# Softmax's division moved from GpSimd to ScalarE, a short token tile packed into one product, and a new split of the last columns

## The chip, the cores and the metric

The kernel runs on one core of a Trainium2 chip. The metric is the device time of one execution in microseconds (us), the median over several runs. The core has five engines with queues of their own: PE (TensorE, matrix products), DVE (VectorE), ACT (ScalarE), POOL (GpSimd) and SP (SyncE, which here issues every DMA).

## The reference

Three blocks follow each other, for 4 batches of 576 tokens with 512 features:

```
scores = scale * q @ k.T            8 heads of 64; heads 0-3 see a window of 32 tokens,
attn   = softmax(masked scores)     heads 4-7 every 4th of 128 tokens
x      = attn @ v
xk, xr = mu * x + (1 - mu) * x_prev (two sets of mu)
x      = sigmoid(xr @ w_r) * (relu(xk @ w_k)**2 @ w_v)
u      = x + (x.T @ U @ V).T        U is 576 x 32, V is 32 x 576: a mix over tokens
out    = u + relu(u @ w_ch1) @ w_ch2
```

Weights come as 64-bit floats and are turned into 32-bit ones on the chip.

## The kernel before, in words

**Order of the work.** Nothing is issued straight away. The builder records operations with the engine, a cost in ns, and the keys that they read and write (op, L124). A planner (plan, L130) then plays the five queues forward, 24 times with ranks from a backward pass, keeps the shortest order, and the operations are issued in that order (L1305 to L1311). Each engine then runs its own list in order. So the costs that the code writes decide which operation stands ahead of which. `lock=True` makes the planner keep a GpSimd and a VectorE operation from overlapping. Where the planner sees TensorE idle for more than 600 ns ahead of a product, it puts matmuls on a tile of zeros there (L279 to L289, issued at L1308), as many as fill 0.7 of the gap at 0.453 ns a column.

**Attention.** 32 units (one pair of heads, one part of the tokens). The first four run alone (attend, L578), the others in twos (attend2, L650), one pair at each "visit" between products of the second block. A unit's scores go to PSUM (qk, L597 or L676), VectorE takes the negated minimum of each group of 64 columns (low, L537), ScalarE the exponential of each group with its row's bias and sum (exp, L546), VectorE the reciprocals of the sums (inv, L551 and L552), GpSimd multiplies all groups by them in one instruction (norm, L557), TensorE transposes (L628, L714), ScalarE copies the transposes out (pts, L632, L720, by the helper at L352), and TensorE multiplies by v (pv, L640, L732). A single unit issues norm twice, for 64 and for 320 columns; a pair issues it once for each head, for 320 or 256 columns.

**Second block.** Chunks of 288 tokens. The first chunk uses whole 32-bit weights (L812, L828), the others split weights and inputs into a high and a low part and do three products for each (L815 to L817). Weights are converted by one ScalarE pass (L385) and four VectorE passes (L386, L387, L389, L392). GpSimd takes the low parts of the inputs (L347).

**Mix over tokens.** For each batch the 576 tokens are five tiles of 128, the last of them only 64 tokens long. y_tr (L902) transposes a tile (L908), ScalarE writes its high part, VectorE its low part. In the short tile GpSimd sets rows 64 to 127 of both parts to zero (L916). u_mm (L919) multiplies each tile's high and low part by U's tile, 512 columns each (L926, L927).

**Third block.** Groups of 256 or 512 tokens. ch1 makes the hidden part (L1036 to L1038), ch2 (L1100) multiplies by w_ch2 into four PSUM banks (L1113 to L1115). After the last step VectorE adds u to each bank (L1133) and SP sends it out (L1136). In the last group the fourth bank is added and sent in two halves of 256 columns, both after the bank's last product.

Of the kernel before, what the change touches and what calls it, by code (L numbers as in the profile page):

```python
# [12 lines left out]
ALU = mybir.AluOpType  # L13
# [3 lines left out]
P = 128  # L17
# [51 lines left out]
SLACK_PE = 100.0  # L69

LATE = 1500.0
FILL, FILL_FROM, FILL_NS = 0.7, 600.0, 0.453
PLAN_PRINT = None
PASSES = 24
RATE = 285.0
# [3 lines left out]
def tile_attention_mix_channel(  # L79
# [18 lines left out]
    def f32(ap):  # L98
        return ap.bitcast(F32)
# [30 lines left out]
    def plan():  # L130
# [149 lines left out]
        for o in order:  # L280
            if o.eng != "PE":
                continue
            for x in [x for x in o.first if x.home is ps][:1] or [k[0] for k in o.w if o.spare][:1]:
                ends = sorted((max(u.done for u in y.ops) for y in x.line[: x.at]), reverse=True)
                room = o.at - max([idle_from, *ends[x.bufs - 1 : x.bufs]])
                if room > FILL_FROM:
                    wide = CW if x in o.first else CW - HS
                    o.before = (x, wide, int(FILL * room / (FILL_NS * wide)))
            idle_from = o.at + o.ns  # L289
        if PLAN_PRINT:  # L290
            PLAN_PRINT(order)
# [44 lines left out]
    def dma(nbytes, fn, r, w):  # L336
        op("SP", 415, fn, r, w, size=nbytes)
# [214 lines left out]
        nc.vector.reciprocal(sm[:, :n], sm[:, :n])  # L552

    def norm(pr, d, sm, i, n, d_to=None):
        src = pr[:, d : d + n * KW].rearrange("p (w k) -> p w k", k=KW)
        dst = src if d_to is None else pr[:, d_to : d_to + n * KW].rearrange("p (w k) -> p w k", k=KW)
        nc.gpsimd.tensor_tensor(out=dst, in0=src, in1=sm[:, i : i + n].unsqueeze(2).to_broadcast([P, n, KW]), op=ALU.mult)  # L557

    LOW, EXP, NORM = 150, 330, 1.69 * KW

    def x_out(ov, q, part, b):

# [15 lines left out]
    def attend(u):  # L578
# [41 lines left out]
        op("DVE", 6 * LOW, lows, [(x,) for x in sc] + [("cst",)], [(pr,), (mn,)], 170)  # L620
        op("ACT", 5 * EXP, exps, [(pr,), (mn,)], [(pr,), (sm,)], 190, mode="exp")
        op("DVE", 260, lambda: inv(sm(), 5), [(sm,)], [(sm,)], 80, lock=True)
        op("POOL", 360 + 6 * NORM, norms, [(pr,), (sm,)], [(pr,)], 40, lock=True)
        yield

        def tr():
# [23 lines left out]
    def attend2(ua, ub):  # L650
# [33 lines left out]
        for e in range(2):  # L684
            first_, own = (ns - 4, 0) if e else (0, 4)
            base = e * ns * KW

            def lows(e=e, first_=first_, own=own, base=base):
                for i in range(4):
                    low(sc[e](), i * KW, pr(), base + (first_ + i) * KW, mk[i // 2], mn[e](), first_ + i)  # L690
                if nw == 10:
                    for f in range(2):
                        low(sc[f](), (4 + e) * KW, pr(), base + own * KW, mk[2], mn[e](), own, head(f))

            def exps(e=e, base=base):
# [206 lines left out]
    def y_tr(b, t, tag):  # L902
        n = min(P, S - t * P)
        pt = bank(tag)

        def tr():
            for p in range(NPAIR):
                nc.tensor.transpose(pt()[:n, p * P : (p + 1) * P], yb[b]()[:, p, t * P : t * P + n], ident)  # L908

        pe(4 * 108, tr, [(yb[b],), ("cst",)], [(pt,)], "tr")  # L910
        hi, lo = Lazy([P, DM], F32R, "w32", "yh", 3), Lazy([P, DM], F32R, "w32", "yl", 3)
        copy(DM, lambda: hi()[:n], lambda: pt()[:n], [(pt,)], [(hi,)], psum=True)
        sub("DVE", DM, lambda: lo()[:n], lambda: pt()[:n], lambda: f32(hi()[:n]), [(pt,), (hi,)], [(lo,)], psum=True)
        if n < P:
            for x in (hi, lo):
                op("POOL", 250, lambda x=x: nc.gpsimd.memset(f32(x()[n:]), 0.0), [], [(x, "rest")], 40)  # L916
        yhl[b, t] = (hi, lo, P)

    def u_mm(b, t, tag):  # L919
        if t == 0:  # L920
            uacc[b] = bank(tag)
        acc = uacc[b]
        hi, lo, n = yhl.pop((b, t))
# [5 lines left out]
        pe(2 * 233, run, [(hi,), (lo,), (hi, "rest"), (lo, "rest")] + [("us", g) for g in range(4)], [(acc,)], "f32r", 400)  # L929
# [166 lines left out]
        return hh, hl, [(t, key) for t in (hh, hl) for key in "io"]  # L1096

    accs = {}

    def ch2(g, j, hid):  # L1100
        hh, hl, kh = hid
        t0, n = GROUPS[g]
        if j == 0:
            accs[g] = [bank("S") for _ in range(4)]
        for o in range(4):
            acc = accs[g][o]

            def run(o=o, acc=acc):
                a = acc()[:, :n]
                for e in range(2):  # L1110
                    wh, wl = (t()[:, o * P : (o + 1) * P] for t in rows2_w[2 * j + e])
                    xh, xl = (t()[:, e * n : (e + 1) * n] for t in (hh, hl))
                    nc.tensor.matmul(a, lhsT=wh, rhs=xh, start=(j == 0 and e == 0), stop=False)  # L1113
                    nc.tensor.matmul(a, lhsT=wl, rhs=xh, start=False, stop=False)  # L1114
                    nc.tensor.matmul(a, lhsT=wh, rhs=xl, start=False, stop=(j == 7 and e == 1))  # L1115

            pe(6 * (MMW if g else MMQ), run, [(t,) for e in range(2) for t in rows2_w[2 * j + e]] + kh, [(acc,)], "f32r")
        if j < 7:
            return
        last = g == len(GROUPS) - 1  # L1120
        for o in range(4):
# [4 lines left out]
            else:  # L1126
                dma(P * n * 4, lambda o=o, ot=ot: nc.sync.dma_start(ot(), uf[:, o, t0 : t0 + n]),
                    [("uf", c, o) for c in range(t0 // HS, (t0 + n - 1) // HS + 1)], [(ot,)])
                u_, ku = ot, (ot,)
            step = Q if last and o == 3 else n  # L1130
            for c0 in range(0, n, step):
                c = slice(c0, c0 + step)
                dve(step, lambda acc=acc, ot=ot, u_=u_, c=c: nc.vector.tensor_tensor(  # L1133
                    out=ot()[:, c], in0=acc()[:, c], in1=u_()[:, c], op=ALU.add),
                    [(acc,), ku], [(ot, c0) if last else (ot,)], two=True, psum=True)
                dma(P * step * 4, lambda o=o, ot=ot, c=c: nc.sync.dma_start(  # L1136
                    out[o, :, t0 + c.start : t0 + c.stop], ot()[:, c]), [(ot, c0) if last else (ot,)], [("out", g, o, c0)])


# [263 lines left out]
```

## Time and profile before

| what | value |
|---|---|
| median of 3 runs | 758.99 us (758.56 to 760.91) |
| the profiled execution | 759.92 us |
| its span in the trace | 758.1 us |
| PE, DVE, ACT, POOL busy, share of the span | 98%, 75%, 52%, 51% |

The profiled execution is one run of the program with the profiler on. Its span is the time from the first to the last record, and the rest of its time lies around the span. Busy time of an engine is the union of its records; a matmul's record includes its way through the array, so 98% for PE says that a product was under way nearly always, and not how dense the products were. Starts of neighbouring products say that.

### The profile page before, as it was taken

How to read it: one execution, taken by the hardware profiler on the slowest of the kernel's cores; microseconds unless marked ns; L12 is line 12 of the kernel's file. 1: busy time of each engine (PE TensorE's matmuls, PEld its weight loads, DVE VectorE, ACT ScalarE, POOL GpSimd, SP SyncE). 2: the span in 40 equal slices, each digit the busy share in tenths (PEclk: the TensorE clock that was granted, in tenths of full speed). 3: DMA queues.
4: the chain of work that ended last, by engine and by line, in shares of the span. 5: the costliest groups of instructions: out<-in, count | busy, mean ns of one | idle time of the engine just before them, and what ended most of it. 6: DMA issues, size and time to landing. Idle time of an engine off the chain costs nothing.

```text
span 758.1 us, 18341 instructions
## 1 busy us (share of the span) xinstructions
PE 739.3 (98%) x6921; PEld 677.6 (89%) x6921; DVE 567.9 (75%) x1335; ACT 393.1 (52%) x995; POOL 388.3 (51%) x408
## 2 busy tenths in 40 slices
PE   8899999999999999999999999999999999999997
PEld 6667999999999999999999998888988989898986
DVE  5999989999898845775677778675888765575632
ACT  4578795767585746372555454343453434343310
POOL 1331464646464635273765677544677554456500
PEclk9999999999999999999999999999999999999999
DMA  9767346776756540557543252132532212042001
GB/s 333 238 255 246 133 148 192 267 248 202 267 179 205 176 157 1 196 160 225 178 153 100 94 181 100 57 125 83 171 102 84 85 56 84 29 140 70 15 1 55
DMA packets 53223, 109.77 MB, mean 145 GB/s; under 512 B 5648, under 2 KB 15888, under 8 KB 53136
## 3 DMA queue, kind: packets, MB, share of 16 engines
q1 hardware_dynamic: 53136, 108.62, 43.4%
q8 instruction: 54, 0.88, 0.5%
q14 instruction: 33, 0.27, 0.1%
HBM read 86.05 MB, written 22.54 MB: 143 GB/s over the span
## 4 chain that ended last, share of the span: by engine, by line
PE 83%; DVE 7%; POOL 3%; issue 3%; DMA 3%; ACT 1%; SPq 0%; DVEq 0%; POOLq 0%; ACTq 0%
PE psM L815 10%; PE psM L816 9%; PE psM L817 9%; PE psS L1115 8%; PE psS L1113 8%; PE psS L1114 8%; PE psM L1036 7%; PE psM L1037 6%; PE psM L1038 6%; PE psM L812 4%; PE psS L732 2%; PE psS L676 1%; DMA uf<-us 1%; POOL cl L347 1%; DVE ok L1073 1%
## 5 line engine op out<-in xcount | busy, mean ns | idle before, releaser
L347 POOL TENSOR_TENSOR cl<-sums,ch 128x512 fp32r<-128x512 f32 x72 | 98.6, 1369 | 93.5 <-ACT ch L352 62.4
L1113 PE MATMUL psS<-hh,rh 128*128 128x512 f32 (+1 forms) x320 | 119.3, 373 | 1.8 <-DVE us L949 1.5
L1115 PE MATMUL psS<-hl,rh 128*128 128x512 f32 (+1 forms) x320 | 119.4, 373 | 0.4 <-DVE hl L1051 0.3
L1114 PE MATMUL psS<-hh,rl 128*128 128x512 f32 (+1 forms) x320 | 118.9, 372 | 0.0
L352 ACT ACTIVATE ch<-sums 128x512 fp32r<-128x512 f32 (+1 forms) x104 | 57.5, 562 | 104.7 <-DVE sums L472 97.0
L815 PE MATMUL psM<-xk,wh 128*128 128x288 f32 x336 | 101.7, 303 | 0.0
L816 PE MATMUL psM<-xk,wl 128*128 128x288 f32 x336 | 99.5, 296 | 0.0
L817 PE MATMUL psM<-xk,wh 128*128 128x288 f32 x336 | 99.3, 295 | 0.0
L347 POOL TENSOR_TENSOR cl<-st,ch 128x256 fp32r<-128x256 f32 x80 | 66.9, 852 | 50.9 <-PE psM L1038 34.7
L472 DVE TENSOR_TENSOR sums<-st 128x256 f32<-128x256 f32 (+1 forms) x144 | 86.2, 646 | 7.8 <-POOL cl L347 3.9
L347 POOL TENSOR_TENSOR xk<-m,xk 128x288 fp32r<-128x288 f32 x56 | 54.8, 992 | 36.2 <-ACT xk L352 18.8
L1115 PEld LDWEIGHTS psS<-hl,rh 128*128 128x128 f32 x320 | 60.3, 188 | 12.3 <-DVE hl L1093 1.0
L1113 PEld LDWEIGHTS psS<-hh,rh 128*128 128x128 f32 x320 | 60.3, 188 | 11.7 <-DVE us L949 1.7
L1114 PEld LDWEIGHTS psS<-hh,rl 128*128 128x128 f32 x320 | 60.3, 188 | 9.4
L815 PE MATMUL psM<-k2s,wh 128*128 128x288 f32 x224 | 67.2, 300 | 0.0
L816 PE MATMUL psM<-k2s,wl 128*128 128x288 f32 x224 | 66.1, 295 | 0.2 <-issue 0.2
L817 PE MATMUL psM<-k2s,wh 128*128 128x288 f32 x224 | 66.0, 295 | 0.0
L815 PEld LDWEIGHTS psM<-xk,wh 128*128 128x128 f32 x336 | 63.5, 189 | 0.7 <-DVE wl L349 0.2
L347 POOL TENSOR_TENSOR k2s<-k,k2s 128x288 fp32r<-128x288 f32 x49 | 45.1, 926 | 36.7 <-ACT k2s L352 34.2
L816 PEld LDWEIGHTS psM<-xk,wl 128*128 128x128 f32 x336 | 63.7, 190 | 0.1
L817 PEld LDWEIGHTS psM<-xk,wh 128*128 128x128 f32 x336 | 63.7, 190 | 0.0
L1093 DVE SCALAR_TENSOR_TENSOR hl<-ort,hh 128x512 fp32r<-128x512 f32 x32 | 26.0, 811 | 46.3 <-ACT hh L1092 46.2
(152 smaller groups left out, 2137.1 us busy)
## 6 DMA issues: line engine op xcount, KB each, us to landing
st<-w2f SPq DMA_DIRECT2D x96, 256.0 KB, 3.1
w<-w2raw SPq DMA_DIRECT2D x32, 512.0 KB, 5.1
w<-w1raw SPq DMA_DIRECT2D x20, 512.0 KB, 5.7
w2f<-w SPq DMA_DIRECT2D x32, 256.0 KB, 2.6
raw<-qk SPq DMA_DIRECT2D x16, 320.0 KB, 6.4
ytmp<-y SPq DMA_DIRECT2D x32, 144.0 KB, 2.6
yb<-ytmp SPq DMA_DIRECT2D x4, 1152.0 KB, 6.8
uf<-us SPq DMA_DIRECT2D x32, 144.0 KB, 1.9
```

Source lines behind the costliest of these rows:

```text
L347: op("POOL", t, lambda: nc.gpsimd.tensor_tensor(out=out_(), in0=a(), in1=b(), op=ALU.subtract), r, w, 40, lock=True)
L352: act(n, lambda: nc.scalar.activation(out_(), in_(), AF.Copy), r, w, psum, strided)
L472: dve(k * Q, lambda: nc.vector.tensor_tensor(out=q(sm_, n, k)(), in0=a(), in1=b(), op=op_), [(s1,), (s2,)], [(sm_, key)], two=True)
L815: nc.tensor.matmul(a, lhsT=wh, rhs=xh, start=start, stop=False)
L816: nc.tensor.matmul(a, lhsT=wl, rhs=xh, start=False, stop=False)
L817: nc.tensor.matmul(a, lhsT=wh, rhs=xl, start=False, stop=stop)
L1036: nc.tensor.matmul(a, lhsT=wh()[:, wi], rhs=xh()[:, ci], start=(k == 0), stop=False)
L1037: nc.tensor.matmul(a, lhsT=wl()[:, wi], rhs=xh()[:, ci], start=False, stop=False)
L1038: nc.tensor.matmul(a, lhsT=wh()[:, wi], rhs=xl()[:, ci], start=False, stop=(k == len(parts) - 1))
L1113: nc.tensor.matmul(a, lhsT=wh, rhs=xh, start=(j == 0 and e == 0), stop=False)
L1114: nc.tensor.matmul(a, lhsT=wl, rhs=xh, start=False, stop=False)
L1115: nc.tensor.matmul(a, lhsT=wh, rhs=xl, start=False, stop=(j == 7 and e == 1))
```

## The change

- The division: norm now issues one ScalarE copy per group of 64 columns, with the reciprocal as the copy's per-row scale. A single unit has 6 such copies, a pair's head 5 or 4. The planner counts 180 ns for one, on ACT; GpSimd has no part in it and the lock with VectorE falls away.
- The short token tile: its high part stays in rows 0 to 63, its low part is written to rows 64 to 127 of the same tile, and U's last 64 rows stand twice in U's tile. One product replaces two, and the zeros of L916 are gone.
- The end: in the last step of the last group the fourth bank's products are done for columns 0 to 383 and then for 384 to 511, and each part is added and sent by itself.
- Fill-in matmuls take 0.6 of a gap instead of 0.7, and half as many ahead of 7 us of the planner's time.

```diff
-FILL, FILL_FROM, FILL_NS = 0.7, 600.0, 0.453
+FILL, FILL_FROM, FILL_NS, FILL_COLD = 0.6, 600.0, 0.453, 7000.0
...
-                    o.before = (x, wide, int(FILL * room / (FILL_NS * wide)))
+                    pace = FILL_NS * (2 if o.at < FILL_COLD else 1)
+                    o.before = (x, wide, int(FILL * room / (pace * wide)))
...
-        nc.gpsimd.tensor_tensor(out=dst, in0=src, in1=sm[:, i : i + n].unsqueeze(2).to_broadcast([P, n, KW]), op=ALU.mult)
-    LOW, EXP, NORM = 150, 330, 1.69 * KW
+        for w in range(n):
+            to = (d if d_to is None else d_to) + w * KW
+            nc.scalar.activation(
+                pr[:, to : to + KW], pr[:, d + w * KW : d + (w + 1) * KW], AF.Copy, scale=sm[:, i + w : i + w + 1])
+    LOW, EXP, NORM = 150, 330, 180
...
-        op("POOL", 360 + 6 * NORM, norms, [(pr,), (sm,)], [(pr,)], 40, lock=True)
+        op("ACT", 6 * NORM, norms, [(pr,), (sm,)], [(pr,)], 140)
...
-            op("POOL", 180 + ns * NORM, lambda e=e, base=base: norm(pr(), base, sm[e](), 0, ns), kp + ks, kp, 40, lock=True)
+            op("ACT", ns * NORM, lambda e=e, base=base: norm(pr(), base, sm[e](), 0, ns), kp + ks, kp, 140)
...
-        sub("DVE", DM, lambda: lo()[:n], lambda: pt()[:n], lambda: f32(hi()[:n]), [(pt,), (hi,)], [(lo,)], psum=True)
-        if n < P:
-            for x in (hi, lo):
-                op("POOL", 250, lambda x=x: nc.gpsimd.memset(f32(x()[n:]), 0.0), [], [(x, "rest")], 40)
-        yhl[b, t] = (hi, lo, P)
+        to, rows = (lo, slice(0, n)) if n == P else (hi, slice(n, P))
+        sub("DVE", DM, lambda: to()[rows], lambda: pt()[:n], lambda: f32(hi()[:n]), [(pt,), (hi,)], [(to, "lo")], psum=True)
+        yhl[b, t] = (hi, lo) if n == P else (hi,)
...
-            nc.tensor.matmul(acc(), lhsT=us[:n, t, :], rhs=hi()[:n], start=(t == 0), stop=False)
-            nc.tensor.matmul(acc(), lhsT=us[:n, t, :], rhs=lo()[:n], start=False, stop=(t == NT - 1))
+            for i, y in enumerate(parts):
+                nc.tensor.matmul(acc(), lhsT=us[:, t, :], rhs=y(), start=(t == 0 and i == 0), stop=(t == NT - 1))
...
+    ENDS = ((0, 3 * Q // 2), (3 * Q // 2, 2 * Q))
...
-        for o in range(4):
+        end = g == len(GROUPS) - 1 and j == 7
+        for o, (c0, c1) in [(o, c) for o in range(4) for c in (ENDS if end and o == 3 else ((0, n),))]:
...
-            step = Q if last and o == 3 else n
-            for c0 in range(0, n, step):
+            for c0, c1 in ENDS if last and o == 3 else ((0, n),):
...
-    up[:S] = um
+    up[:S], up[S:] = um, um[S - NT * P :]
```

## Rows read from the trace of the kernel before

**Rows 1.** The page's busy times: engine, us (share of the span), instructions.

```profile
PE 739.3 (98%) x6921; PEld 677.6 (89%) x6921; DVE 567.9 (75%) x1335; ACT 393.1 (52%) x995; POOL 388.3 (51%) x408
```

**Rows 2.** Stretches: length, busy PE, PEld, DVE, ACT, POOL (count), granted clock, DMA share, GB/s.

```profile
12.00:16.00 4.00, 4.00 (x78) 2.90 (x74) 3.90 (x15) 3.06 (x15) 0.66 (x1) 1.00 1.03 390
...
20.00:40.00 20.00, 16.46 (x275) 12.40 (x274) 19.12 (x64) 11.94 (x40) 7.16 (x9) 1.00 0.81 256
...
60.00:80.00 20.00, 19.96 (x308) 15.88 (x315) 18.21 (x58) 16.84 (x45) 6.71 (x9) 1.00 0.78 250
...
100.00:104.00 4.00, 4.00 (x129) 3.79 (x122) 3.54 (x21) 4.00 (x12) 2.61 (x4) 0.61 0.51 132
```

**Rows 3.** Waits of PE: waiter, releaser, us in total, times, longest.

```profile
PE psS L628 <- POOL pr L557: 1.5, 2, 0.9
PE psS L732 <- ACT pts L352: 1.4, 1, 1.4
PE psS L714 <- POOL pr L557: 0.8, 1, 0.8
PE psS L927 <- POOL yl L916: 0.7, 1, 0.7
```

**Rows 4.** The chain that ended last, 0 to 56 us: start, us, what.

```profile
1.46 4.10 PE psS L1308 x9
...
20.85 0.81 DVE wx L386
...
33.90 0.77 DVE wx L386
...
45.66 10.22 PE psM L812 x40
```

**Rows 5.** Timeline of DVE and POOL, 24 to 30 us: start, us, engine, line.

```profile
24.57 0.42 DVE L386 TENSOR_SCALAR wx<-wx 128x512 f32<-128x512 f32 x1
...
28.20 0.84 DVE L386 TENSOR_SCALAR wx<-wx 128x512 f32<-128x512 f32 x1
...
27.67 1.09 POOL L557 TENSOR_TENSOR pr<-pr,sm 128x64 f32<-128x64 f32 x2 [0.33 <-DVE sm L552]
```

**Rows 6.** Groups: line, engine, operation, count | busy us, mean ns | idle before.

```profile
L546 ACT ACTIVATE pr<-pr,mn 128x64 f32<-128x64 f32 x144 | 48.1, 336 | 8.7 <-DVE mn L537 7.2 <-POOL pr L557 1.3
...
L352 ACT ACTIVATE ch<-st 128x256 fp32r<-128x256 f32 x80 | 28.7, 404 | 6.4 <-PE psM L816 4.1 <-PE psM L1038 2.3
...
L557 POOL TENSOR_TENSOR pr<-pr,sm 128x320 f32<-128x320 f32 (+2 forms) x36 | 26.3, 732 | 60.3 <-DVE sm L552 42.3 <-ACT wx L385 7.9 <-ACT pr L546 3.9
...
L352 ACT ACTIVATE rh<-st 128x512 fp32r<-128x512 f32 x16 | 9.7, 621 | 4.6 <-DMA st<-w2f 4.6
...
L926 PE MATMUL psS<-yh,us 128*128 128x512 f32 x10 | 4.1, 412 | 0.0
...
L916 POOL MEMSET yh<- 64x512 f32 x4 | 2.1, 522 | 0.6 <-PE psM L927 0.4
```

**Rows 7.** Timeline of ACT at the first exponentials.

```profile
6.44 0.35 ACT L546 ACTIVATE pr<-pr,mn 128x64 f32<-128x64 f32 x1 [4.41 <-DVE mn L537]
6.69 0.19 ACT L546 ACTIVATION_READ_ACCUMULATOR pr<-pr,mn 128x1 f32 x1
```

**Rows 8.** The first loads: issue, time to landing (last number), and the second unit's scores.

```profile
0.75 0.39 SPq L526 DMA_DIRECT2D raw<-qk  x1
...
raw<-qk SPq DMA_DIRECT2D x1, 320.0 KB, 3.3
...
9.02 0.50 PEld L597 LDWEIGHTS psS<-raw 64*32 64x32 f32 x40 [0.35 <-DMA raw<-qk]
```

**Rows 9.** The end: last piece of PE in the chain, then VectorE's adds and SP's issues.

```profile
753.69 0.24 PE psS L1115
...
753.95 0.76 DVE L1133 TENSOR_TENSOR ot<-psS,ug 128x256 f32<-128x256 f32 x2 [0.70 <-PE psS L1115]
...
753.28 1.94 SPq L1136 DMA_DIRECT2D out<-ot  x3
```

More of the change, by code (lines that the diff above doesn't have):

```diff
@@ L554, in norm @@
     def norm(pr, d, sm, i, n, d_to=None):
-        src = pr[:, d : d + n * KW].rearrange("p (w k) -> p w k", k=KW)
-        dst = src if d_to is None else pr[:, d_to : d_to + n * KW].rearrange("p (w k) -> p w k", k=KW)
-        nc.gpsimd.tensor_tensor(out=dst, in0=src, in1=sm[:, i : i + n].unsqueeze(2).to_broadcast([P, n, KW]), op=ALU.mult)
-    LOW, EXP, NORM = 150, 330, 1.69 * KW
+        for w in range(n):
[3 more added lines that the diff above has]
+    LOW, EXP, NORM = 150, 330, 180
     def x_out(ov, q, part, b):
@@ L922, in u_mm @@
         acc = uacc[b]
-        hi, lo, n = yhl.pop((b, t))
+        parts = yhl.pop((b, t))
         def run():
-            nc.tensor.matmul(acc(), lhsT=us[:n, t, :], rhs=hi()[:n], start=(t == 0), stop=False)
-            nc.tensor.matmul(acc(), lhsT=us[:n, t, :], rhs=lo()[:n], start=False, stop=(t == NT - 1))
-        pe(2 * 233, run, [(hi,), (lo,), (hi, "rest"), (lo, "rest")] + [("us", g) for g in range(4)], [(acc,)], "f32r", 400)
+            for i, y in enumerate(parts):
+                nc.tensor.matmul(acc(), lhsT=us[:, t, :], rhs=y(), start=(t == 0 and i == 0), stop=(t == NT - 1))
+        pe(len(parts) * 233, run, [(parts[0],), (parts[-1], "lo")] + [("us", g) for g in range(4)], [(acc,)], "f32r", 400)
         if t == NT - 1:
@@ L1104, in ch2, with run @@
             accs[g] = [bank("S") for _ in range(4)]
-        for o in range(4):
+        end = g == len(GROUPS) - 1 and j == 7
+        for o, (c0, c1) in [(o, c) for o in range(4) for c in (ENDS if end and o == 3 else ((0, n),))]:
             acc = accs[g][o]
-            def run(o=o, acc=acc):
-                a = acc()[:, :n]
+            def run(o=o, acc=acc, c0=c0, c1=c1):
+                a = acc()[:, c0:c1]
                 for e in range(2):
                     wh, wl = (t()[:, o * P : (o + 1) * P] for t in rows2_w[2 * j + e])
[L1112 to L1117, printed above, removed]
+                    xh, xl = (t()[:, e * n + c0 : e * n + c1] for t in (hh, hl))
+                    nc.tensor.matmul(a, lhsT=wh, rhs=xh, start=(j == 0 and e == 0), stop=False, skip_group_check=c0 > 0)
+                    nc.tensor.matmul(a, lhsT=wl, rhs=xh, start=False, stop=False, skip_group_check=c0 > 0)
+                    nc.tensor.matmul(a, lhsT=wh, rhs=xl, start=False, stop=(j == 7 and e == 1), skip_group_check=c0 > 0)
+            k_acc = [(acc, c0)] if end and o == 3 else [(acc, x) for x, _ in ENDS] if g == len(GROUPS) - 1 and o == 3 else [(acc,)]
+            pe(6 * (3 + 0.4487 * (c1 - c0)), run, [(t,) for e in range(2) for t in rows2_w[2 * j + e]] + kh, k_acc, "f32r")
         if j < 7:
@@ L1129, in ch2 @@
                 u_, ku = ot, (ot,)
-            step = Q if last and o == 3 else n
-            for c0 in range(0, n, step):
-                c = slice(c0, c0 + step)
-                dve(step, lambda acc=acc, ot=ot, u_=u_, c=c: nc.vector.tensor_tensor(
+            for c0, c1 in ENDS if last and o == 3 else ((0, n),):
+                c = slice(c0, c1)
+                dve(c1 - c0, lambda acc=acc, ot=ot, u_=u_, c=c: nc.vector.tensor_tensor(
                     out=ot()[:, c], in0=acc()[:, c], in1=u_()[:, c], op=ALU.add),
-                    [(acc,), ku], [(ot, c0) if last else (ot,)], two=True, psum=True)
-                dma(P * step * 4, lambda o=o, ot=ot, c=c: nc.sync.dma_start(
+                    [(acc, c0) if last and o == 3 else (acc,), ku], [(ot, c0) if last else (ot,)], two=True, psum=True)
+                dma(P * (c1 - c0) * 4, lambda o=o, ot=ot, c=c: nc.sync.dma_start(
                     out[o, :, t0 + c.start : t0 + c.stop], ot()[:, c]), [(ot, c0) if last else (ot,)], [("out", g, o, c0)])
```

## The prediction

> **What bounds the kernel now.** I read the page's busy times first. PE is busy for 98% of the span, the next engine, DVE, for 75% [rows 1]. So whatever the change takes from POOL or puts on ACT matters only where PE waits for them, and the first question is where PE waits at all. The stretches answer that: from 20 to 40 us PE is busy for 16.46 of 20 us and DVE for 19.12, from 60 to 80 us PE for 19.96 [rows 2]. The start is DVE's, and the rest PE's. The list of PE's waits says the same: the longest sums are 1 to 2 us [rows 3]. The chain shows how the start ends: it runs over fill-in matmuls on zeros (4.10 us for 9), DVE's conversion passes (L386 and its neighbours), and at 45.66 us it goes over to PE and stays there [rows 4]. So there are three places to gain: the 45 us of the start, PE work that falls away, and the end behind the last product.
>
> **The change part by part.** All of it is summed against the profiled execution, 759.92 us, which stands 0.93 us (0.1%) above the median of 758.99; the same difference is then put on the median.
>
> *The division on ACT.* It takes 36 instructions and 26.3 us from POOL [rows 6] and gives ACT one copy for each group of 64 columns: 4 single units by 6, 6 pairs by 10 and 8 pairs by 8, which is 148. (The exponentials, counted the same way without the copy that norm makes twice, are 144, as the trace has them [rows 6].) What is one copy? A plain copy takes 404 ns for 256 columns and 621 ns for 512 [rows 6], 0.85 ns a column, so 241 ns for 64. The exponential of 64 columns, which has a per-row operand too, takes 336 ns [rows 6], and what follows it starts 0.25 us after it (6.44 to 6.69) [rows 7], an overlap of 0.10. So a copy occupies 0.14 us (the plain one less that overlap) to 0.336 us. I take 0.25, for the exponential is the nearest row, and the 180 ns that the new code plans with is then too little. That makes 148 × 0.25 = 37 us more on ACT (21 to 50), of which 32 copies or 8 us fall into the start. ACT is busy for 11.94 us of 20 to 40 us and for 16.84 of 60 to 80 us [rows 2], so the cover is there, but thin after 60 us. If it is gone, the pts copies queue behind the divisions and PE's products with v wait; that is a rival below. Copy already stands between exponentials, so I count no further table load.
>
> By the Trainium skill, "ScalarE: Activation LUTs", section "What ACT_TABLE_LOAD costs", a [128,1] operand adds about 93 ns to an activation of 186 ns + 0.833 ns a column. By that a copy of 64 columns would be about 332 ns long, an estimate; the 336 ns of the exponential agree.
>
> *Latency of the division.* On POOL both instructions of one single unit take 1.09 us together [rows 5]; on ACT 6 × 0.25 + 0.10 = 1.6 us. A pair's head takes 5 × 0.25 + 0.1 = 1.35 us instead of about 0.73 [rows 6]. So the division gets slower, not faster. PE's three waits for it (1.5 us at L628, 0.8 us at L714) [rows 3] go over to ACT and grow by up to 0.5 us each. The division also waits for DVE's reciprocals, and behind it on ACT stand the first conversion pass (L385) and pts. Little of this is on the chain, which is mostly DVE there: +0.3 us, between 0 and +1.5.
>
> *VectorE freed of POOL.* Plain L386 takes 0.42 us; the one at 28.20 us, beside a division on POOL (27.67 to 28.76), takes 0.84 [rows 5]. The chain holds two more like it, 0.81 us at 20.85 and 0.77 at 33.90 [rows 4], which I put down to the divisions too. DVE is the chain of the start, so these count: (0.84 + 0.81 + 0.77) − 3 × 0.42 = 1.16, taken as −1.1 us. Twice that is the lower bound, if as much again is hidden in passes not shown, and zero the upper one, if DVE then waits for ACT instead. After 46 us the same relief hides under PE: 0.
>
> *Fewer fill-in matmuls.* The first nine take 4.10/9 = 0.456 us each [rows 4], against 0.24 for a 512-column product at the end [rows 9]: they run at half pace. They end at 5.56 us, but the first unit's operands are there at about 0.75 + 3.3 = 4.05 us [rows 8]. By the new rule some 9 × 0.6/0.7/2 = 4 are left and the first scores can start 1.4 us earlier. Most of that is lost again: the second unit's scores wait for their own load at 9.02 us [rows 8], and from 12 to 16 us the DMA engines are full (share 1.03) [rows 2]. I take −0.5 us. The lower bound is −1.4. The upper one is +1.6, if TensorE falls to its lower clock for lack of work: from 100 to 104 us, just after a wait of PE of 1.4 us for pts [rows 3], the granted clock averages 0.61 [rows 2], so 78% of 4 us ran at 1.2 instead of 2.4 GHz, and half of those 3.1 us is lost.
>
> *The short token tile.* Four products of 512 columns fall away, one for each batch, at 0.24 us pace [rows 9] (the 412 ns of a record [rows 6] are latency): 0.9 us of PE work where PE is the bound. The two POOL fills (L916, about 0.52 us each [rows 6]) go too, and with them the wait of 0.7 us at L927 [rows 3], of which I count 0.6, since the low part from DVE is needed still. Together −1.5 us, between −0.9 and −2.2.
>
> *The end.* PE ends at 753.93 us [rows 9]. Before, two adds of 256 columns follow (0.76 us) and the last issue ends at 753.28 + 1.94 = 755.22 [rows 9]. After, the 384-column add (1.5 × 0.42 = 0.63 us, estimated from one of two adds) starts six 128-column products before PE's end. At a quarter of 0.24 us these last 0.36 us, so the first add ends 0.27 us after PE and one of 128 columns, about 0.2, ends at 0.48 instead of 0.76: −0.3 us. If a 128-column product is no faster than a 384-column one (0.18), PE ends 0.7 us later: +0.4. Lower bound −0.5.
>
> Sum: −0.5 − 1.1 + 0.3 − 1.5 − 0.3 = −3.1 us: 756.8 for such an execution, **755.9 us** for the median.
>
> **The rivals.** *The start keeps its length* (757.2 us). The order is planned anew, loads and reciprocals set the pace, or DVE is stretched by the POOL work that comes next instead of the divisions, so that freeing GpSimd does not free VectorE. For it: the DMA share of 1.03 and the wait of 0.35 us for raw [rows 2, 8]. Against it: DVE's 19.12 of 20 us [rows 2]. Only −1.5 − 0.3 are left.
>
> *ACT takes POOL's place* (761.9 us, slower). A pair's divisions hold ACT for 2.5 us, and behind them stand pts and the first conversion pass. PE has waited for pts once already, 1.4 us [rows 3], and lost another 1.6 to the clock [rows 2]: 3.0 us each. It decides from the second new wait of this kind among the 12 pairs after 46 us: −3.1 + 2 × 3.0 = +2.9. For it: 16.84 of 20 us busy, before 2.5 us are added [rows 2]. Against it: ACT's mean is 52% [rows 1], and the planner counts ACT's new work when it orders.
>
> The rule in the Trainium skill, "ScalarE: Activation LUTs", section "Rules for kernel authors", to multiply on VectorE and not on ScalarE, points the same way; the trace bears it out as far as a division gets longer, and no run yet shows more.
>
> *More falls into place* (751.7 us). The new order also loses the wait for pts and its clock (−3.0), and the start gains 1.2 us more within its bounds: −7.3. For it speaks that this wait is the only long one between 46 and 280 us; against it, that nothing in the change aims there.
>
> **How the numbers follow.** The forecast has 0.44 (its own range 754.6 to 757.0), the unchanged start 0.28, more falling into place 0.15, ACT as bound 0.13. No change is what lies within 0.3% or 2.3 us, about what a measurement of this kernel can tell: 756.7 to 761.3. Faster: 0.40 of the forecast and 0.15 make 0.55. Same: 0.04 and 0.28 make 0.32. Slower: 0.13. The range from 751.5 to 760.5 takes in the first two and most of the third, and leaves out most of ACT as bound.
>
> **What would show it.** Copies at L557's place on ACT starting 0.25 us apart; L386 near 0.42 us throughout the start; the point where PE turns continuous 1 to 2 us before 45.66; 4 products fewer at the mix over tokens and no wait at L927; the last issue 0.3 us closer to PE's end. It is wrong if PE turns continuous no earlier, or if new waits of PE for pts or for the divided scores, with a granted clock under 1 behind them, stand between 46 and 280 us.

## The result, and the profile after

The changed kernel takes **752.37 us** (median of 6 runs, 751.23 to 755.24), the kernel before 758.91 us on the same chip (6 runs). The ratio is 0.9912, with a 95% interval from 0.9890 to 0.9933: 6.7 us faster, between 5.1 and 8.3. The forecast was 3.1 us faster. The profiled execution takes 753.58 us and its span is 751.8 us, 6.3 us less than the 758.1 us of before. All readings below go by spans.

The page's busy times of the changed kernel: engine, us (share of the span), instructions.

```profile
PE 737.1 (98%) x6927; PEld 676.7 (90%) x6927; DVE 552.3 (73%) x1335; ACT 424.7 (56%) x1143; POOL 352.7 (47%) x364
```

Against [rows 1], ACT has the 148 copies more that were counted, and 31.6 us more busy time. POOL has 44 instructions fewer (36 divisions, 8 fills) and 35.6 us less, DVE 15.6 us less with the same instructions. So the work moved as the change says. PE is still busy for 98%, and its waits must tell the rest.

PE's longest waits in the changed kernel: waiter, releaser, us in total, times, longest.

```profile
PE psM L830 <- DVE xk L771: 2.2, 3, 1.3
PE psM L814 <- DVE wx L393: 2.1, 1, 2.1
PE psS L599 <- DMA raw<-qk: 1.5, 1, 1.5
...
PE psS L678 <- issue: 1.0, 2, 0.7
PE psS L642 <- ACT pts L353: 0.5, 1, 0.5
```

Of the waits of [rows 3] those for the division and for the filled rows are gone, and that for pts at L732 (L734 here) is down to 0.2 us. New are one of 2.1 us for a converted weight (L393, L392 before) and one of 1.5 us for the second unit's load. (Line numbers grew by one to four.)

**The start ends earlier.** Timeline of PE in the changed kernel: start, us, engine, line.

```profile
41.80 0.30 PE L678 MATMUL psS<-raw 64*32 64x64 f32 x2 [0.68 <-issue]
42.03 2.21 PE L814 MATMUL psM<-xk,wx 128*128 128x288 f32 x8
```

L814 is L812 before: the products that began at 45.66 us [rows 4] begin at 42.03, 3.6 us earlier.

**And that is given back between 60 and 80 us.** The first chunk's second set of products with whole weights (times in ns, then first and last start), first before and then changed:

```profile
L812 PE MATMUL psM<-k,wx x64: 406/406/510, 64.2 to 82.7; 128*128 128x288 f32 x64
```

```profile
L814 PE MATMUL psM<-k,wx x64: 403/406/684, 61.8 to 85.7; 128*128 128x288 f32 x64
```

It begins 2.4 us earlier and ends 3.0 us later. The chain of the changed kernel there (start, us, what):

```profile
62.42 0.60 DVE wx L393
63.02 0.34 DVE wx L388
63.36 0.09 DVE sm L552
...
63.70 2.50 ACT pr L558 x10
66.19 0.33 ACT xk L353
66.53 0.56 ACT wx L386
67.09 0.33 ACT xk L353
67.42 0.57 ACT wx L386
67.99 0.65 ACT pts L353 x2
...
73.20 1.11 PE psM L1310 x10
74.31 1.48 PE psM L814 x6
...
77.13 0.70 DVE wx L393
77.83 0.04 issue
77.87 7.29 PE psM L814 x22
```

Ten copies of the division hold ACT for 2.50 us, and behind them in its queue stand the first conversion passes of the weights (L386); VectorE waits 1.16 us for the first of these. The copies are not the whole delay. Five of VectorE's passes between 67 and 74 us meet a subtraction on GpSimd and take 2.2 us longer together than their fellows, as here:

```profile
69.60 1.05 POOL L348 TENSOR_TENSOR xk<-m,xk 128x288 fp32r<-128x288 f32 x1 [1.27 <-ACT xk L353]
```

```profile
69.91 1.02 DVE L388 TENSOR_SCALAR wx<-wx 128x512 int32<-128x512 int32 x1
```

And a pair's minima (L538) stand ahead of the last pass on VectorE, from 74.98 to 77.1 us. PE runs out of converted weights, takes ten fill-ins at 73.20, and goes on at 77.87, when the last conversion is done. Stretches of the changed kernel there, with PE's busy time, granted clock and DMA share:

```profile
74.00:78.00 4.00, 1.90 (x10) 1.00 0.79 270
78.00:82.00 4.00, 4.00 (x10) 0.57 0.94 280
```

After the wait TensorE is granted 0.57 on the mean over 4 us, mostly its 1.2 GHz level instead of 2.4: 86% of 4 us at half pace, which costs 1.7 us more. Before, it was the wait for pts near 98 us that had this tail [rows 2]. In the changed kernel that wait and its tail are gone, and from the last of these products to the first landmark below it takes 203.2 us, where the kernel before takes 205.6.

**Where the 6.3 us come from.** Four landmarks cut the span: the first product of the mix over tokens (L926 before, L927 after), the first product of the mix for the third batch (the same line into psM), the last one, and the end. They are the first and last starts of the instructions that read tile yh. First the kernel before:

```profile
L926 PE MATMUL psS<-yh,us x10: 387/396/496, 288.3 to 343.7; 128*128 128x512 f32 x10
L926 PE MATMUL psM<-yh,us x10: 392/396/401, 405.7 to 508.2; 128*128 128x512 f32 x10
```

and the changed kernel:

```profile
L927 PE MATMUL psS<-yh,us x10: 387/396/476, 288.9 to 341.4; 128*128 128x512 f32 x10
L927 PE MATMUL psM<-yh,us x10: 391/394/401, 401.4 to 501.7; 128*128 128x512 f32 x10
```

Up to the first landmark, which has all of the softmax in it, the changed kernel is 0.6 us *later* (288.9 against 288.3). From there to the third batch it takes 112.5 us against 117.4, from there to the last product of the mix 100.3 against 102.5, and to the end 250.1 against 249.9. So 0.6 − 4.9 − 2.2 + 0.2 = −6.3: in these two executions **all of the gain is made around the mix over tokens**, where the packed tile is, and none where the division is. (Of the −2.2, 0.7 us is work that moved: six products of 256 columns of the third block, 0.12 us apart, stand ahead of the last product of the mix in the kernel before and behind it in the changed one.)

One place there shows how. After the mix, VectorE adds each product with V to x into a buffer with two halves (us, L949), SP writes a half to memory (uf), and a half can be filled again only when its transfer has landed. First the chain of the kernel before:

```profile
356.10 8.40 DMA uf<-us
364.62 0.47 DVE us L949
365.13 0.39 PE psS L1113
```

The 8.40 us transfer holds up the last addition, and PE waits for that:

```profile
PE psS L1113 <- DVE us L949: 1.5, 1, 1.5
```

The eight additions run from 347.7 to 364.6 us, 16.9 us, in the kernel before and from 345.4 to 359.4, 14.0 us, in the changed one, whose longest such transfer takes 5.4 us. PE's busy time in 140 us from 300 on, first before:

```profile
300.00:440.00 140.00, 136.39 (x1024) 1.00 0.50 159
```

and changed:

```profile
300.00:440.00 140.00, 139.68 (x1062) 1.00 0.50 164
```

3.61 us of idle time became 0.32.

### The profile page after: what moved, and what is told of

It is laid out like the page before. It is cut to its first block, busy times and chain, and to the rows that moved or that the text cites. A ratio compares the mean times of both kernels' runs of the same rounds, so it can differ in the third digit from the quotient of the medians.

```text
span 751.8 us, 18408 instructions
## 1 busy us (share of the span) xinstructions
PE 737.1 (98%) x6927; PEld 676.7 (90%) x6927; DVE 552.3 (73%) x1335; ACT 424.7 (56%) x1143; POOL 352.7 (47%) x364
## 4 chain that ended last, share of the span: by engine, by line
PE 84%; DVE 5%; ACT 3%; issue 1%; DMA 1%; POOL 0%; DVEq 0%; SPq 0%; ACTq 0%
PE psM L817 9%; PE psM L819 9%; PE psM L818 9%; PE psS L1117 8%; PE psS L1115 8%; PE psS L1116 8%; PE psM L1036 8%; PE psM L1038 8%; PE psM L1037 8%; PE psM L814 3%; PE psS L734 2%; PE psS L678 1%; DVE sums L473 1%; DMA ug<-uf 1%; PE psS L716 1%
## 5 line engine op out<-in xcount | busy, mean ns | idle before, releaser
L1117 PE MATMUL psS<-hl,rh 128*128 128x512 f32 (+2 forms) x322 | 119.8, 372 | 0.2
L1115 PE MATMUL psS<-hh,rh 128*128 128x512 f32 (+2 forms) x322 | 119.3, 371 | 0.2 <-ACT hh L1092 0.2
L1116 PE MATMUL psS<-hh,rl 128*128 128x512 f32 (+2 forms) x322 | 119.3, 370 | 0.0
L819 PE MATMUL psM<-xk,wh 128*128 128x288 f32 x336 | 99.0, 295 | 0.0
L348 POOL TENSOR_TENSOR xk<-m,xk 128x288 fp32r<-128x288 f32 x56 | 52.4, 946 | 80.1 <-ACT xk L353 55.1
L348 POOL TENSOR_TENSOR cl<-st,ch 128x256 fp32r<-128x256 f32 x80 | 64.7, 825 | 52.5 <-PE psM L1038 36.9
L473 DVE TENSOR_TENSOR sums<-st 128x256 f32<-128x256 f32 (+1 forms) x144 | 82.5, 623 | 6.6 <-POOL cl L348 5.5
L1115 PEld LDWEIGHTS psS<-hh,rh 128*128 128x128 f32 x322 | 60.7, 189 | 9.9 <-ACT hh L1092 0.6
L819 PE MATMUL psM<-k2s,wh 128*128 128x288 f32 x224 | 66.1, 295 | 0.3 <-POOL xk L348 0.3
L1093 DVE SCALAR_TENSOR_TENSOR hl<-ort,hh 128x512 fp32r<-128x512 f32 x32 | 28.7, 898 | 47.9 <-ACT hh L1092 47.9
L819 PEld LDWEIGHTS psM<-xk,wh 128*128 128x128 f32 x336 | 63.2, 188 | 0.1
```

Source lines behind the costliest of these rows:

```text
L348: op("POOL", t, lambda: nc.gpsimd.tensor_tensor(out=out_(), in0=a(), in1=b(), op=ALU.subtract), r, w, 40, lock=True)
L473: dve(k * Q, lambda: nc.vector.tensor_tensor(out=q(sm_, n, k)(), in0=a(), in1=b(), op=op_), [(s1,), (s2,)], [(sm_, key)], two=True)
L819: nc.tensor.matmul(a, lhsT=wh, rhs=xl, start=False, stop=stop)
```

## The experiments

Three accounts were to be told apart (the expectations name theirs by letters of their own and say what each means). By the parts (theory F), each part of the change is worth its own instructions and waits. By the order (theory C), the planner writes another order for each kernel, since costs and operations change, and the time follows which order it finds. By ScalarE as the new bound (the rival of the prediction), the copies cost more than GpSimd's single instruction did. The table has all kernels, in microseconds of their profiled executions but for the median and ratio. Column A is the first landmark, B the stretch to the third batch, C that to the mix's last product; D is the start of the last pass that converts a weight of the first chunk (L392, L393 or the line that stands for it), and E is PE's idle time from 300 to 440 us. Differences to the kernel before are worked out from the ratio (a ratio of 0.9931 is 5.2 us of 758), those to the changed kernel from the medians. The latter carry up to 1 us more of doubt, since the kernels were timed on several chips, on which the kernel before has medians from 757.94 to 758.91 us.

```
kernel             division  tile    order      median  ratio   A      B      C      D     E
before             GpSimd    padded  before's   758.91  1       288.3  117.4  102.5  71.7  3.61
n3_fill_alone      GpSimd    padded  before's   757.33  0.9988  286.7  116.5  102.7  71.4  2.96
n4_end_alone       GpSimd    padded  before's   758.05  1.0000  288.9  117.3  102.6  72.3  3.88
n11_b_cost160      GpSimd    padded  new        763.38  1.0065  292.8  116.2  102.1  70.7  2.78
n1_div_alone       ScalarE   padded  new        762.87  1.0050  292.4  117.9  101.6  75.1  3.66
n6_no_tile         ScalarE   padded  new        765.93  1.0094  294.6  115.2  101.6  74.2  2.57
n7_old_order       ScalarE   padded  before's   766.46  1.0113  296.1  115.9  102.7  75.0  2.45
n12_tile_old_order GpSimd    packed  before's   756.31  0.9966  288.2  114.2  102.1  72.0  1.99
n2_tile_alone      GpSimd    packed  new        753.16  0.9931  289.8  111.3  100.4  72.2  0.00
n5_no_div          GpSimd    packed  new        755.50  0.9962  292.5  111.2  100.3  73.7  0.16
n8_new_order_pool  GpSimd    packed  after's    756.35  0.9971  295.7  110.9  100.2  82.2  0.00
after              ScalarE   packed  after's    752.37  0.9912  288.9  112.5  100.3  77.1  0.32
n9_cost250         ScalarE   packed  new        751.66  0.9910  287.8  110.7  100.2  74.7  0.00
n10_cost170        ScalarE   packed  new        752.94  0.9924  289.9  111.2  100.1  75.5  0.38
```

The order of n3 and n4 is before's: their traces have the instructions of VectorE, ScalarE and GpSimd in the same sequence as the kernel before. Columns A to E come from one execution of each kernel, and executions of one kernel differ: those of the kernel before run from 756.97 to 761.83 us on one chip, and the profiled ones lie up to 3.3 us below (n6) and 2.7 us above (n4) their kernel's median. The four kernels in before's order with the division on GpSimd have A from 286.7 to 288.9, so 2 us of A tell little.

**The packed tile alone.** Only the part of the change in the mix over tokens, on the kernel before:

```diff
-        yhl[b, t] = (hi, lo, P)
...
+        yhl[b, t] = (hi, lo) if n == P else (hi,)
...
-    up[:S] = um
+    up[:S], up[S:] = um, um[S - NT * P :]
```

> The kernel before with the packed token tile alone. Theory A: 4 to 6 us faster, and no wait of TensorE for a load or an add at 360 to 380 us. Theory B: 1.5 us faster, 0.9 from four products fewer and 0.6 from the wait for the zeros. Theory C: any value.

Measured: 753.16 us, ratio 0.9931 (0.9912 to 0.9951), 5.2 us faster, over three times the 1.5 us of the prediction. The table places it: B is 111.3 against 117.4 and C 100.4 against 102.5, together 8.2 us less, while A is 1.5 us later. In PE's waits of this kernel the longest sum is one that the profile puts down to no engine:

```profile
PE psS L676 <- issue: 4.1, 3, 1.6
```

**The packed tile in the old order.** The instructions keep the order of the kernel before; the four products and eight fills that are no longer needed are left out of it.

```diff
             for x in (hi, lo):
-                op("POOL", 250, lambda x=x: nc.gpsimd.memset(f32(x()[n:]), 0.0), [], [(x, "rest")], 40)
...
+                op("POOL", 250, lambda: None, [], [(x, "rest")], 40)
...
+        parts = (hi, lo) if n == P else (hi,)
```

> The kernel before with the packed token tile in the old order: four products and eight fills are left out, everything else stands where it stood. If the work that falls away is the gain: 1.5 to 3 us faster (0.9 of TensorE, the wait for the zeros, and what hangs on the earlier end of the tile). If the new order is the gain: no more than 1.5 us faster, and the 1.5 us wait at L1113 still there. If the earlier tile alone frees the entry of the third block: 4 to 6 us faster.

Measured: 756.31 us, ratio 0.9966 (0.9953 to 0.9979), 2.6 us faster, near the size of the sum in the prediction. The wait for the fills at L927 is gone, and that for us became shorter, as the transfers begin earlier (346.7 us against 348.2), but it is still there: 1.5 us at L1113 before, 0.7 here (PE psS L1115 <- DVE us L951). The tile is not all that sets this wait: with the padded tile it goes from 0.5 us (the division in the old order, below) to 1.9 (the end alone). So of the 5.2 us of the tile alone, about half is the work left out, and about half comes with the new order. That the order could be as good with the padded tile is unlikely by columns B and C: no padded kernel, in four orders, comes near the packed ones.

**The division alone.** The copies and their costs on the kernel before, planned anew:

```diff
-        nc.gpsimd.tensor_tensor(out=dst, in0=src, in1=sm[:, i : i + n].unsqueeze(2).to_broadcast([P, n, KW]), op=ALU.mult)
...
+        for w in range(n):
+            to = (d if d_to is None else d_to) + w * KW
+            nc.scalar.activation(
+                pr[:, to : to + KW], pr[:, d + w * KW : d + (w + 1) * KW], AF.Copy, scale=sm[:, i + w : i + w + 1])
...
-    LOW, EXP, NORM = 150, 330, 1.69 * KW
...
+    LOW, EXP, NORM = 150, 330, 180
...
-        op("POOL", 360 + 6 * NORM, norms, [(pr,), (sm,)], [(pr,)], 40, lock=True)
+        op("ACT", 6 * NORM, norms, [(pr,), (sm,)], [(pr,)], 140)
```

> The kernel before with the division on ScalarE alone. Theory A (the gain of the change is made where the third block begins, 300 to 380 us, by the packed token tile): within 2 us of the kernel before, with the lead of the start lost again by 80 us. Theory B (the gain is VectorE's in the start, as forecast): 1 to 3 us faster, and the lead still there at 300 us. Theory C (the gain comes from a new order of the work as a whole): any value, and the parts will not add up to 6.5 us.

Measured: 762.87 us, ratio 1.0050 (1.0032 to 1.0068), 3.8 us *slower*, which neither A nor B allowed. PE's waits there, the longest and the two that bear on the question:

```profile
PE psS L715 <- ACT pr L557: 1.8, 6, 0.7
...
PE psS L733 <- ACT pts L352: 1.1, 1, 1.1
...
PE psS L1114 <- DVE us L950: 1.0, 1, 1.0
```

Six waits for the divided scores and one for pts: PE now waits for ACT where it waited for POOL, as the rival said, in small pieces. But in sum they are no longer than before: all waits for divided scores come to 2.2 us against 2.3, and those for pts to 1.4 against 2.5. So the listed waits do not account for the 3.8 us, and what does is not shown.

**The division in the old order.** The same copies, but planned with GpSimd's costs, so that every instruction stays at its place:

> The kernel before with the division's copies on ScalarE, at the very place in the order that the planner had found for GpSimd (its costs and queues as before). Theory D: 3 to 5 us slower than before, as with its own order. Theory E: within 2 us of before.

Measured: 766.46 us, ratio 1.0113 (1.0091 to 1.0134), 8.6 us slower, more than both theories allowed. PE's waits:

```profile
PE psM L813 <- ACT sg L352: 2.9, 2, 1.8
PE psM L816 <- DVE k L863: 2.7, 4, 1.0
PE psS L733 <- ACT pts L352: 2.4, 3, 1.6
PE psS L629 <- ACT pr L557: 2.1, 1, 2.1
```

What stands behind the copies on ACT comes late: sg, the root of k for VectorE's square, one of the pts. (The waits for the division itself stay at 2.1 us, 2.3 before.) The division's latency and the time of its copies in ACT's queue, which no run separates, have a real price, 7.8 us up to the first landmark (296.1 against 288.3), where it was summed as +0.3.

**The changed kernel with the division back on GpSimd,** planned anew:

> The changed kernel with the division back on GpSimd, planned for it; tile, fill and end as changed. Theory D (the division costs 4 to 5 us in company as it does alone): 747 to 749 us, faster than the changed kernel. Theory E (in company it costs nothing, since its loss alone came from the order that the planner found for it): 752 to 754 us.

Measured: 755.50 us, ratio 0.9962 (0.9945 to 0.9979), above both theories. Beside the 752.37 us of the full change the division on ScalarE is worth 3.1 us here (3.8 by the ratios), after costing 3.8 us alone. B and C are those of the packed tile. The difference is in A, 292.5 against 288.9, and "issue" waits of PE come to 4.2 us there (1.0 in the changed kernel). The order is another one too, so this is not the price of the division by itself.

**The changed kernel's own order, division on GpSimd.** One instruction at the place of the copies, nothing else moved:

```diff
-        for w in range(n):
-            to = (d if d_to is None else d_to) + w * KW
-            nc.scalar.activation(
-                pr[:, to : to + KW], pr[:, d + w * KW : d + (w + 1) * KW], AF.Copy, scale=sm[:, i + w : i + w + 1])
...
+        nc.gpsimd.tensor_tensor(out=dst, in0=src, in1=sm[:, i : i + n].unsqueeze(2).to_broadcast([P, n, KW]), op=ALU.mult)
```

> The changed kernel in its own written order, instruction for instruction, but each softmax division is again one instruction on GpSimd, at the place in the order where ScalarE's copies stood. Theory A (ScalarE's copies themselves cost time and were only bearable by the order around them): without them 748 to 751 us. Theory B (the order was laid out for ScalarE's copies, and a division that takes 0.8 us of GpSimd and the shared port comes late for its products in it): 755 to 760 us. Neither: within 1.5 us of 752.4.

Measured: 756.35 us, ratio 0.9971 (0.9956 to 0.9986), 4.0 us over the changed kernel. Theory B is borne out and theory A falls. Instructions of the weights' last pass (count, ns, first and last start) in this kernel,

```profile
L393 DVE SCALAR_TENSOR_TENSOR wx<-w,wx x10: 650/684/1149, 49.6 to 82.2; 128x512 int32<-128x512 int32 x10
```

and in the changed one:

```profile
L393 DVE SCALAR_TENSOR_TENSOR wx<-w,wx x8: 651/686/1150, 51.9 to 77.1; 128x512 int32<-128x512 int32 x8
```

Its A is 295.7, 6.8 us later. Together with the division in the old order this is a symmetric result: either engine in an order that was laid out for the other costs 7 to 8 us up to the first landmark.

**The changed kernel with the old short tile,** planned anew:

> The changed kernel with the old token tile (zeros on GpSimd, two products). Theory D: 761 to 763 us, the division's loss without the tile's gain. Theory E: 757 to 759 us, as before. Both want TensorE's waits at 300 to 380 us back.

Measured: 765.93 us, ratio 1.0094 (1.0069 to 1.0119), 13.6 us over the changed kernel and above both theories. Only part of that is the tile. B and C are 4.0 us longer. But A is 5.7 us later too, and up to there the two kernels execute the same operations, fill-ins aside: that is order, and the scatter of single executions. The profiled execution, of 762.60 us, was this kernel's fastest, so the remaining 3.3 us to its median have no trace.

**The fill-ins alone and the end alone.**

```diff
-FILL, FILL_FROM, FILL_NS = 0.7, 600.0, 0.453
+FILL, FILL_FROM, FILL_NS, FILL_COLD = 0.6, 600.0, 0.453, 7000.0
...
-                    o.before = (x, wide, int(FILL * room / (FILL_NS * wide)))
+                    pace = FILL_NS * (2 if o.at < FILL_COLD else 1)
+                    o.before = (x, wide, int(FILL * room / (pace * wide)))
```

> The kernel before with fewer fill-in matmuls alone; the order of all other work is that of before. Theory A and C: 0 to 0.7 us faster. Theory B: 0.5 us faster, the first scores at about 4 us instead of 5.5. If the lower clock bites, up to 1.6 us slower.

Measured: 757.33 us, ratio 0.9988 (0.9971 to 1.0005). The interval holds both the 0.5 us of the prediction and no gain. PE's start in this kernel:

```profile
1.46 2.07 PE L1309 MATMUL psS<-zero 128*128 128x512 f32 x4 [1.46 <-DVE zero L1305]
3.63 0.90 PE L598 MATMUL psS<-raw 64*32 64x64 f32 x40
4.47 3.42 PE L1309 MATMUL psS<-zero 128*128 128x512 f32 x10
9.08 0.66 PE L598 MATMUL psS<-raw 64*32 64x64 f32 x40 [1.20 <-DMA raw<-qk]
```

Four fill-ins in place of nine, as worked out, and the first scores at 3.63 us, 0.4 earlier than the landing at 4.05 that the prediction counted with; but the second unit's scores wait for their own load and start at 9.08, where they started at 9.02 before [rows 8].

```diff
+    ENDS = ((0, 3 * Q // 2), (3 * Q // 2, 2 * Q))
...
+        for o, (c0, c1) in [(o, c) for o in range(4) for c in (ENDS if end and o == 3 else ((0, n),))]:
...
-            for c0 in range(0, n, step):
+            for c0, c1 in ENDS if last and o == 3 else ((0, n),):
```

> The kernel before with the last bank split into 384 and 128 columns alone. All theories: 0.3 us faster, seen as less time between TensorE's last product and the last issue; 0.4 slower if a product of 128 columns costs as much as one of 384.

Measured: 758.05 us, ratio 1.0000 (0.9986 to 1.0014). The interval, 1.1 us either way, cannot tell the forecast 0.3 us from nothing; the traces can. The end of the changed kernel shows that nothing is gained. PE's last products and VectorE's adds there:

```profile
747.15 0.34 PE L1117 MATMUL psS<-hl,rh 128*128 128x384 f32 x1
...
747.83 0.28 PE L1117 MATMUL psS<-hl,rh 128*128 128x128 f32 x1
748.14 0.76 DVE L1135 TENSOR_TENSOR ot<-psS,ug 128x384 f32<-128x384 f32 x2 [0.97 <-PE psS L1117]
```

The product that completes the 384 columns ends at 747.49, but the add of these columns starts only at 748.14, when PE has finished the whole bank. The two adds take 0.76 us behind PE's end, exactly as the two equal ones did [rows 9]. The last issue ends 1.4 us behind PE (747.21 + 2.33 against 748.12), where it ended 1.3 behind it before.

**The same instructions at another price.** The last three kernels change one number that the planner reads, and no instruction, fill-ins aside.

```diff
-    LOW, EXP, NORM = 150, 330, 180
+    LOW, EXP, NORM = 150, 330, 250
```

> The changed kernel with the planner's price of a normalisation copy on ScalarE raised from 180 to 250 ns (the pace that the trace shows); the same instructions in another order. Theory C (a good part of the gain is the order that the planner happened on): it lies 3 us or more from 752.4. Theory F (the gain is in the parts themselves): within 1.5 us of 752.4. Were the low price a fault that costs time, 749 to 751 us.

Measured: 751.66 us, ratio 0.9910 (0.9891 to 0.9930), within 0.7 us of the changed kernel.

> The changed kernel with the planner's price of a normalisation copy lowered from 180 to 170 ns; the same instructions in another order. Theory C (order): 3 us or more from 752.4, more likely above, 754 to 762 us. Theory F (parts): within 1.5 us of 752.4.

Measured: 752.94 us, ratio 0.9924 (0.9907 to 0.9941), within 0.6 us. For the changed kernel theory F is borne out and theory C falls, as far as three orders can show it: one time for all. The three A are 288.9, 287.8 and 289.9, though the places differ: at 250 ns D is 2.4 us earlier and the wait for converted weights is gone, but PE waits 1.7 us for "issue" and 2.7 for pts instead.

> The kernel before with the planner's price of the division on GpSimd lowered by a twentieth (1.60 in place of 1.69 ns per column and unit); the same instructions in another order. Theory C (order): 3 us or more from 758.8, either way. Theory F (parts): within 1.5 us of 758.8.

Measured: 763.38 us, ratio 1.0065 (1.0050 to 1.0080), 4.9 us slower. For the kernel before theory C is right: A is 292.8 against 288.3, B and C are 1.6 us shorter. The products that came in at 45.66 us come in at 39.2:

```profile
L812 PE MATMUL psM<-xk,wx x64: 404/407/510, 39.2 to 57.4; 128*128 128x288 f32 x64
```

That is earlier than in the changed kernel, with the division on GpSimd as it was. Neither theory holds alone, and the columns say which holds where. **A is order**: it runs from 286.7 to 296.1 us, and neither engine is ahead in it. The seven kernels with the division on GpSimd in an order laid out for it, padded and packed, lie between 286.7 and 292.8 (four of them have before's order, 286.7 to 288.9), the five with ScalarE in an order laid out for that between 287.8 and 294.6. **B and C are the tile**: 115.2 to 117.9 and 101.6 to 102.7 with the padded one in seven kernels, 110.7 to 112.5 and 100.1 to 100.4 with the packed one in the six that were planned with it, and 114.2 and 102.1 with it in the old order.

## Why the prediction was right, and where it was wrong

The direction and the range came out: 752.37 us lies in 751.5 to 760.5, but below the forecast's own range of 754.6 to 757.0. Two terms of the sum were off in opposite ways, and the end's term came to nothing. That the time still fell into the range is luck in part.

- **The short token tile (−1.5) was mis-sized.** It gives −2.6 us in the old order, just beyond its lower bound of −2.2, −5.2 alone and planned anew, and in the changed kernel B and C fall by 7.1, of which 0.7 is work that moved. The step that failed is the bound: it counted the tile's own products, fills and wait, and not what stands behind them. PE's 3.6 us of idle time from 300 to 440, among it 1.5 us at L1113 behind an 8.40 us transfer, were in the trace, one stage after the place that was read. The waits and their share were looked up for the lines of the diff only.
- **VectorE freed of POOL (−1.1): the passes got shorter, but what follows from that did not come.** The first pass (L387, L386 before) takes 0.42 us each time from 18 to 41 us, and the products come in 3.6 us earlier, not 1 to 2. But these 3.6 us are the new order's. With the copies on ScalarE in the old order the products come in at 48.1 us, 2.4 later than before, and with the division still on GpSimd in new orders at 41.1 (n5), 40.1 (n2) and 39.2 (n11, which only has another price). And at the first landmark nothing is left. The step that failed is the end of the start: the chain went over to PE at 45.66 us [rows 4] (after a wait of 1.6 us for sg, a copy on ACT, which the rows leave out), and all behind it was put down as hidden under PE. But the weights' conversion goes on to 72 us, on VectorE and ScalarE both, and is the next thing to be late. With ScalarE's copies it ends later in every one of the six kernels that have them (D from 74.2 to 77.1 us, against 70.7 to 73.7 with GpSimd in an order of its own), and in the old order, where nothing else changed, by 3.3 us.
- **Latency of the division (+0.3, up to +1.5) was too low.** In the old order it is 7.8 us by A, with the copies' time in ACT's queue in it and what VectorE gained already taken off, and 4.1 in a new order, part of which is the order's own spread. The price of a copy was right: ten take 2.50 us and start 0.24 apart, where 0.25 was taken. Their mean length is 338 ns. By the Trainium skill, "ScalarE: Activation LUTs", section "What ACT_TABLE_LOAD costs", neighbours overlap by about 93 ns. By that a copy of 338 ns takes the queue for 245, an estimate, and the 0.24 us of the trace agree.
- **The rival that the start keeps its length** was right in its result, and for two of the reasons that it gave: the order is planned anew, and VectorE is stretched by GpSimd's next work, 2.2 us between 67 and 74 us. It was worth 757.2 us with the tile at its forecast size.
- **The rival that ACT takes POOL's place** is what happens in the old order; with the division alone the waits went over to ACT, but did not grow. In the changed kernel its pattern came once: not pts, but the weights behind the copies, 2.1 us of waiting and 1.7 us of clock, against the 3.0 us that were set for one such wait. One does not decide.
- **The rival that more falls into place** (751.7 us) came nearest in time, and half of it came: the wait for pts near 98 us and its tail are gone. But a wait for weights with a tail of its own took their place, the start's gain was gone by the first landmark, and the time came from the mix, which this rival did not name. That its number fits is luck.
- **Fewer fill-ins (−0.5)**: −0.9, between −2.2 and +0.4, is not distinguishable from it.
- **The end (−0.3)** was wrong in its step that the first add starts before PE's end. It came out at zero. The small products run 0.11 us apart, not at a quarter of 0.24, so six of them and six of 384 columns (0.17) take 1.68 us where six of 512 took 1.40.

By landmarks, in one execution of each, the forecast's parts up to the mix sum to −0.5 − 1.1 + 0.3 = −1.3, where +0.6 came; its tile is −1.5, where −7.1 came; its end is −0.3, where +0.2 came. The first part was forecast 1.9 us too short and the tile's 5.6 us too long.

## What to carry to other kernels

When an operation falls away where the tensor engine is the bound, follow the stage it belongs to until the next stage runs, and look there for waits on buffers and transfers that begin earlier when it is gone; the products themselves may be the smaller part. An engine that becomes free early may gain nothing if the next operand is late for another reason, here an engine that was just given more to do, and the order of the queues: read which operand is late next, not when the bound changes hands. Where a planner writes the order, compare parts in landmarks and not in totals, and time one kernel with a price changed by a few per cent before believing a difference of half a per cent.

## What the runs showed of the hardware

- **A wait that nothing releases.** PE stops for up to 1.9 us ahead of a run of scores (L676 to L678) or of a split product (L815 to L819), and the profile names "issue", which is time in which the engine waited for nothing that it shows. It is 0.2 us in the kernel before, 1.0 in the changed one, 1.0 to 1.7 in five others and 4.1 or 4.2 in three (n2, n5, n6). It differs from order to order, and in one order too (0.2 in the kernel before, 1.0 in n12). What it is was not settled.
- **A wait can have a tail at the lower clock, and need not.** Before, the granted clock fell after a wait of 1.4 us for pts near 98 us; now it falls after one of 2.1 us for weights near 76 us. It costs 1.6 us there (as worked out in the prediction) and 1.7 here. But in the kernel before the granted clock stays at 1.00 behind a wait of 1.6 us that ends at 45.66 us, and behind the one of 1.5 us at L1113.
- **VectorE beside GpSimd.** From 18 to 46 us in the changed kernel, seven of eight first passes take 0.42 or 0.43 us. The eighth, beside GpSimd's subtraction, takes twice that:

```profile
40.90 1.65 POOL L348 TENSOR_TENSOR d<-x 128x288 f32<-128x288 f32 x2 [4.43 <-ACT x L353]
```

```profile
39.62 0.42 DVE L387 TENSOR_SCALAR wx<-wx 128x512 f32<-128x512 f32 x1
41.15 0.88 DVE L387 TENSOR_SCALAR wx<-wx 128x512 f32<-128x512 f32 x1
```

By the Trainium skill, "SBUF — State Buffer", section "SBUF: two separate sides", a GpSimd instruction and a VectorE instruction in a two-port mode lock the port pair that they share: the one that starts first has it for its whole instruction, and the other blocks. The traces agree as to the blocking: this pass ends 0.28 us after the first of the two subtractions (41.75 us). In the kernel before and the changed one together, 17 first and second passes (L386 and L387 before) start while GpSimd multiplies or subtracts, and 14 of them end 0.28 or 0.29 us after its instruction, however early they started. (The other three start shortly before its end and end up to 0.39 us after it.) In which mode the passes run the traces do not show.

- **An add waits for its whole bank.** The add of 384 columns started 0.02 us after PE's last product into the same bank, though its own columns were complete 0.65 us before. Whether that is the program's wait or the memory's was not tried.
